# Attention and a channel MLP on one core: v's load, the mixing's staging tiles, V's low part and the pace of weight conversion rearranged

## The chip, the cores and the metric

One core of one Trainium2 chip runs the whole program. The metric is device time in microseconds. Engines: PE is TensorE (PEld its weight loads), DVE VectorE, ACT ScalarE, POOL GpSimd, SP SyncE, which here only issues DMAs. Each engine runs its instructions in program order.

## The reference

Inputs are q, k, v (4 x 8 heads x 576 x 64), a small network w1, b1, w2 for the positional bias, and for the second half U (576 x 32), V (32 x 576), w_ch1 (512 x 2048) and w_ch2 (2048 x 512) in 64-bit floats. All arithmetic is to be good to about float32.

```python
scores = q @ k.T / 8 + bias            # bias[h, i, j] = relu(x[i, j] * w1 + b1) @ w2, the same for every batch
attn = softmax(scores)                 # divided by (sum + 1e-9)
x = (attn @ v) as (4, 576, 512)
h = x.T @ U @ V                        # mixing over the sequence, rank 32
u = x + h.T
out = u + relu(u @ w_ch1) @ w_ch2
```

where x[i, j] = log1p(|i - j|) / log1p(max(i, 1)).

## The kernel before, in words

Products that need float32 precision are made of two parts of 32-bit floats, a rounded high part and the rest, its low part: high*high + high*low + low*high. So every operand is split once, a cast for the high part and a subtraction for the low part.

**Bias stage.** The bias is made first, in 36 steps of 16 rows each (list `order`): `bias_hid` writes four hidden tiles, one on ACT and three on DVE (L312, L314), from a ring of ten slots; `bias_mm` multiplies them on PE; `bias_out` scales the result on ACT into one of eight ring slots (L336) and SP issues two or four DMAs from there to the bias tiles. Four of these eight slots lie in the space of x_sb. Into these steps are set the splits of the first two pairs of heads (`prep_ops(p, True)`: cast on ACT L195, subtraction on DVE L201), the raw loads of pair 1 (`second`), the loads of v, and the first scores, bias adds and exponentials of pair 0 (dictionary `early`). After the steps a memset of 64 rows of x_sb on POOL (L913) waits until the ring's slots in x_sb are read out.

**Attention.** There are 16 pairs of heads, p = 0 to 15, four to a batch. A pair takes one run through the string table SLOTS, nine slots s = 0 to 8 written by hand, in which every name is one step: S scores on PE, T bias add with row minimum on DVE (L385), E exponential on ACT (L403), X and C transposes of P and their copies, I and CI the same for the middle rows, PM `norm_m` (the normalised middle rows, L424 on POOL; for p = 0 on ACT, L422), AV the product with v, A and D assembling x_sb. One prime on a name means the pair before, two the one before that. Q1 to Q4 on POOL split the next pair's q and k (L197, L201); LA and LB issue the raw loads of pair p + 2 on SP. `load_v(p + 1)` is issued at slot 7 of pair p, into one of two v tiles; the tile is free when the step AV1'' of slot 0 has run.

**Conversion.** U, V and the first quarter of the MLP's weights are converted from 64-bit words in 20 jobs, two a pair from pair 2 on (VA, VD, VS, VJ, VP in SLOTS): two ACT steps, three DVE steps (L224, L229, L235), one POOL addition (L240), then a finishing step, which `convert` runs at the next job's VP. For V (three jobs, `fin_v`) this is a cast on ACT (L798) and a DVE instruction (L799) that leaves the high part in some groups of 32 rows and the low part in the others. Converted weights go to DRAM and come back late (`first_weights`, L929, steps listed in FEED).

**Mixing.** When the four pairs of a batch are done, the mixing of that batch runs inside the next pair (p = 5, 9, 13): MT to MX make the rank-32 products, H0 to H4 the five products with V, HD0 to HD4 (`mix_add`, L600) add x_sb into a staging tile y, U0 to U4 (`mix_store`, L604) store it to u_dram. The staging tiles are three, th, tl and y, in turn. The fourth batch's mixing runs in the transition behind the last pair.

**MLP.** u_dram comes back in 18 tiles acc of 128 rows, nine blocks of 256 rows. `make_ut` transposes a block on PE and splits it (ACT L721, DVE L727); `mlp1(n)` makes the hidden layer in four steps and splits it (L763, L764); `mlp2(n)` has two steps, accumulates into acc (L784) and in the last round stores. Weights are handled in four quarters, so there are four rounds of nine blocks (n = 0 to 35). In rounds 1 to 3 the next quarter's weights are converted in `background`: `pipeline` turns 16 jobs into 51 groups of instructions, and after every step of the MLP two groups are issued. All PSUM accumulators come from four tiles of two banks.

The functions of kernel and helpers that the change touches:

Of the kernel before, what the change touches and what calls it, by code (L numbers as in the profile page):

```python
# [20 lines left out]
DM = H * D  # L21
# [25 lines left out]
    "S1 HD3' U3' T1 VA0",  # L47
    "S2 T2 X20' H4' Q1 VP1' Q2 LA C20' HD4' U4'",
    "S3 T3 PM H1' H0' X30' Q3",
# [16 lines left out]
def kernel(  # L66
# [50 lines left out]
    three, mask = consts[:, 2:3].bitcast(I32), consts[:, 3:4].bitcast(I32)  # L117
    low = consts[:, 4:5]
    u_sb = mix.tile([P, 5, RANK], F32, name="u_sb")
# [64 lines left out]
    def prep_ops(p, early=False):  # L184


        hi = qkp.tile([P, 2 * KD * TB], F32R, tag="hi", name="hi")
        lo = qkp.tile([P, QKW], F32R, tag="lo", name="lo")
        qk_ops[p] = (hi, lo)

        parts = [(raws[p, 0], hi[:, 0:QQ], lo[:, 0:QQ]), (raws[p, 1], hi[:, QQ:QKW], lo[:, QQ:QKW])]

        def high(raw, h, l):
            if early:
                nc.scalar.copy(out=h, in_=raw)  # L195
            else:
                nc.gpsimd.tensor_scalar(out=h, in0=raw, scalar1=1.0, scalar2=0.0, op0=ALU.mult, op1=ALU.add)  # L197

        def low(raw, h, l):
            eng = nc.vector if early else nc.gpsimd  # L200
            eng.tensor_tensor(out=l, in0=raw, in1=h.bitcast(F32), op=ALU.subtract)  # L201

        return [lambda o=o, i=i: o(*parts[i]) for i in range(2) for o in (high, low)]
# [49 lines left out]
    small_sb = tabp.tile([P, 33], F32, name="small_sb")  # L253
    extra = tabp.tile([P, S], F32, name="extra")
    psi = tabp.tile([P, S // 32, STEP], F32, name="psi")
# [159 lines left out]
    def norm_m(p):  # L415
# [3 lines left out]
        for o, i, n in ((0, 0, S), (S, S - LEFT, LEFT)):  # L419
            src = d["praw"][:, i : i + n]  # L420
            if p == 0:
                nc.scalar.activation(out=pm[:, o : o + n], in_=src, func=AF.Copy, scale=rec)  # L422
            else:
                nc.gpsimd.tensor_scalar(  # L424
                    out=pm[:, o : o + n], in0=src, scalar1=rec, scalar2=1.0, op0=ALU.mult, op1=ALU.mult
                )

# [119 lines left out]
    mixt = {}  # L547
    stages = cycle(("th", "tl", "y"))

# [47 lines left out]
    def mix_add(c):  # L597
        n = P if c < 4 else LEFT
        y = mixt["y", c] = mix.tile([P, DM], F32, tag=next(stages), name="y")
        nc.vector.tensor_tensor(out=y[0:n], in0=mixt[c][0:n], in1=x_sb[0:n, c, :], op=ALU.add)  # L600
# [6 lines left out]

    conv = {}

    def convert(what, k, p):  # L610
# [12 lines left out]
        elif what == "J":  # L623
            join()
            if j + 3 < len(conv["jobs"]):
                conv["jobs"][j + 3][0]()
        else:
            if j:
                conv["jobs"][j - 1][2]()
            add()  # L630
            if j == len(conv["jobs"]) - 1:
                fin()
# [163 lines left out]
    def fin_v(a, e):  # L796
        def fin(y):
            nc.scalar.copy(out=vq[:, a:e], in_=y)  # L798
            nc.vector.scalar_tensor_tensor(  # L799
                out=vq[:, a:e], in0=vq[:, a:e].bitcast(F32), scalar=low, in1=y, op0=ALU.mult, op1=ALU.add  # L800
            )

# [47 lines left out]
    nc.gpsimd.memset(eps, 1.0e-9)  # L850
    nc.gpsimd.memset(low, 0.0)
    for r in (RANK, 3 * RANK):
        nc.gpsimd.memset(low[r : r + RANK], -1.0)
    load_pair(0)
# [22 lines left out]
    order = [32, 33, 34, 35] + [8 * c + i for c in range(4) for i in (0, 4, 1, 5, 2, 6, 3, 7)]  # L877
    early = {12: 0, 22: 1, 23: 2, 30: 3, 31: 4, 36: 5, 37: 6}
    preps[-1] = prep_ops(0, True)
    second = pair_loads(1)  # L880
    for i in range(len(order) + 3):
# [10 lines left out]
        if 2 <= i < len(order) + 2:  # L892
            bias_out(order[i - 2])
        if i == 25:
            preps[0] = prep_ops(1, True)
        if 5 <= i < 9 or 25 <= i < 29:
            preps[-1 if i < 9 else 0].pop(0)()
        if i in (12, 14, 16, 18, 20, 22):
            second.pop(0)()
        if i == 15:  # L900
            load_v(0)
        if i - 1 in early:
            first(f"E{early[i - 1]}")
        if i - 1 == 12:
            first("N0")
        if i in early:
            first(f"S{early[i]}", f"T{early[i]}")
    load_v(1)
    done.update((f"Q{i}", 0) for i in range(1, 5))
# [28 lines left out]
    for p in range(NP):  # L938
        if p > 0:
            new_pair(p)  # L940
        for s in range(9):
            if s == 7 and 0 < p < NP - 1:
                load_v(p + 1)
            if p == CONV_FROM - 1 and s in (0, 2, 4):
# [29 lines left out]

    period(NP, 0)
    for i in range(6, 9):
# [6 lines left out]
    make_ut(0, 0)  # L983
    period(NP, 1)
    make_ut(0, 1)
    run(m[0][0])
    t = [qkp.tile([P, QKW], F32R, tag="lo", name="ut") for _ in range(2)]
# [28 lines left out]
    for i, c in enumerate((4, 0, 1, 2, 3)):  # L1016
        run((m[2][1:] + y[1])[i])
        last_mix(c)
    p1.close()

# [14 lines left out]
    for n in range(2, NG * NB + 1):  # L1035
# [7 lines left out]
        if g + 1 < NG and (n == 2 or (j == 0 and g > 0)):  # L1043
            queue += pipeline(weight_jobs(g + 1, split))
            queue[1:1] = [[]] * 8
        steps = []
        if n + 1 < NB:
            steps += [lambda i=i: make_ut(n + 1, i) for i in range(TT)]
        if 2 < n < NG * NB:
            steps += mlp1(n)  # L1050
        if n > 2:
            steps += mlp2(n - 1)
        for o in steps:
            o()
            background(2)

# [69 lines left out]
```

## Time and profile before

| | |
|---|---|
| median of 3 runs | 745.96 us (742.02 to 750.25) |
| the profiled execution | 745.49 us, span 743.5 us |
| PE busy, share of the span | 696.8 us, 94% |
| DVE, ACT, POOL busy | 60%, 48%, 28% |
| mean granted TensorE clock | 0.982 |
| bias stage, with pair 0's first scores | 5.3 to about 76 us |
| attention, pairs 1 to 15 | to about 309 us |
| transition to the MLP | to about 355 us |
| MLP, conversion of the second quarter beside it | 354.9 to 434.4 us |
| MLP, the three rounds left | to 743.5 us |

The span is from the first to the last instruction. PE's busy time has the overlap of its pipelined matmuls modelled, so a stage at 100% is a stage in which PE never waits, at whatever clock.

### The profile page before, as it was taken

Reading aid. Unit: us, or ns where it says so; the run is one execution under the profiler, and the core shown is the slowest. Engines: PE = TensorE matmul, PEld = TensorE weight load, DVE = VectorE, ACT = ScalarE, POOL = GpSimd, SP = SyncE. Lnnn points to the kernel's source line nnn. Section 1 sums busy time; section 2 is a strip of 40 time slices with the busy share of each in tenths; the row PEclk is TensorE's granted clock in tenths of the full one; section 3 lists DMA queues with packets and bytes.
Section 4 is the critical chain, followed back from the end, with each engine's and each line's share of the span. In section 5 each row is a group of like instructions: output and inputs, shape, how many; then the busy total and the mean of one; then the engine's idle time right before and its main releaser. Section 6 shows DMA issues by size and latency. Waiting matters only on the chain.

```text
span 743.5 us, 16699 instructions
## 1 busy us (share of the span) xinstructions
PE 696.8 (94%) x6708; PEld 573.4 (77%) x6708; DVE 447.4 (60%) x932; ACT 358.7 (48%) x769; POOL 207.8 (28%) x225
## 2 busy tenths in 40 slices
PE   6978898889999998899899999999999999999998
PEld 4434676657766776687787989989989989989986
DVE  7977698879988877334598328842268622222222
ACT  7978798769987987631355114421044211011010
POOL 0000565445664645200166005520036400000000
PEclk9999999999999999999999999999999999999999
DMA  5687645454554454301533002310013000011111
GB/s 131 190 209 205 155 120 141 112 155 127 162 163 124 124 140 153 118 2 50 202 100 106 6 1 88 91 50 1 1 55 102 30 1 1 1 42 43 57 44 71
DMA packets 39885, 68.25 MB, mean 92 GB/s; under 512 B 5888, under 2 KB 12544, under 8 KB 39808
## 3 DMA queue, kind: packets, MB, share of 16 engines
q1 hardware_dynamic: 39424, 67.01, 31.0%
q8 instruction: 53, 0.87, 0.5%
q14 instruction: 24, 0.20, 0.1%
q10 hardware_dynamic: 384, 0.18, 0.1%
HBM read 45.02 MB, written 11.53 MB: 76 GB/s over the span
## 4 chain that ended last, share of the span: by engine, by line
PE 76%; DMA 6%; DVE 6%; ACT 4%; issue 3%; SPq 2%; POOL 2%; DVEq 0%; POOLq 0%; ACTq 0%
PE ph L758 25%; PE po L781 25%; PE o L505 10%; PE sc L370 7%; PE tb L447 3%; DMA bias<-ring 2%; DMA u_dram<-y 2%; PE bs L321 2%; PE tx L447 1%; DVE ring L314 1%; DMA raw<-in_qk_dram 1%; PE ti L447 1%; ACT ring L312 1%; DVE wt L235 1%; DVE wt L229 1%
## 5 line engine op out<-in xcount | busy, mean ns | idle before, releaser
L763 ACT ACTIVATE hh<-ph 128x1024 fp32r<-128x1024 f32 x36 | 36.9, 1025 | 203.3 <-PE ph L758 203.3
L764 DVE SCALAR_TENSOR_TENSOR hh<-ph,hh 128x1024 fp32r<-128x1024 f32 x36 | 44.1, 1225 | 139.1 <-ACT hh L763 139.1
L240 POOL TENSOR_TENSOR wy<-wt,wy 128x256 int32<-128x256 int32 (+1 forms) x68 | 52.5, 772 | 234.8 <-DVE wt L235 197.0
L781 PE MATMUL po<-bias,hh 128*128 128x512 f32 x432 | 102.1, 391 | 0.0
L403 ACT ACTIVATE p<-p,st 128x576 f32<-128x576 f32 x128 | 98.3, 771 | 2.9 <-DVE st L385 2.9
L781 PE MATMUL po<-wq,hh 128*128 128x512 f32 x360 | 98.1, 394 | 0.0
L385 DVE CUSTOM_DVE_ANT_0 p<-sc,bias 128x576 f32<-128x576 f32 x128 | 92.6, 750 | 8.4 <-PE sc L370 4.7
L505 PE MATMUL o<-pt,v 128*64 128x320 f32 (+1 forms) x640 | 87.8, 422 | 5.1 <-DVE y L600 5.1
L781 PEld LDWEIGHTS po<-bias,hh 128*128 128x128 f32 x432 | 79.8, 188 | 16.2
L781 PEld LDWEIGHTS po<-wq,hh 128*128 128x128 f32 x360 | 66.6, 188 | 14.3
L505 PEld LDWEIGHTS o<-pt,v 128*64 128x64 f32 x640 | 44.3, 141 | 36.1 <-DVE y L600 5.5
L758 PE MATMUL ph<-ut,bias 128*128 128x256 f32 x512 | 67.5, 280 | 2.7 <-DVE bias L784 2.7
L758 PEld LDWEIGHTS ph<-ut,bias 128*128 128x128 f32 x512 | 63.8, 189 | 3.6 <-issue 3.1
L758 PE MATMUL ph<-ut,wq 128*128 128x256 f32 x512 | 65.0, 276 | 0.0
L758 PEld LDWEIGHTS ph<-ut,wq 128*128 128x128 f32 x512 | 62.0, 188 | 1.0
L201 POOL TENSOR_TENSOR lo<-raw,hi 128x1152 fp32r<-128x1152 f32 (+1 forms) x28 | 59.3, 2117 | 1.5
L370 PE MATMUL sc<-hi 64*128 64x288 f32 (+1 forms) x320 | 57.1, 349 | 2.7 <-DVE y L600 1.9
L321 PE MATMUL bs<-ring,small_sb 128*32 128x256 f32 (+2 forms) x780 | 50.6, 367 | 8.4 <-ACT ring L312 7.3
L430 ACT COPY pt<-tb 128x1024 f32<-128x1024 f32 x48 | 47.9, 1012 | 16.1 <-PE tb L447 16.1
L784 DVE TENSOR_TENSOR acc<-po,acc 128x512 f32<-128x512 f32 x36 | 24.9, 691 | 46.4 <-PE po L781 46.4
L758 PE MATMUL ph<-bias 128*128 128x256 f32 x352 | 51.1, 290 | 1.2 <-ACT bias L721 0.7
L370 PE MATMUL sc<-lo,hi 64*128 64x288 f32 (+1 forms) x320 | 49.2, 299 | 0.6 <-POOL lo L201 0.6
(110 smaller groups left out, 1217.2 us busy)
## 6 DMA issues: line engine op xcount, KB each, us to landing
wraw<-in_w_ch_dram SPq DMA_DIRECT2D x64, 256.0 KB
raw<-in_qk_dram SPq DMA_DIRECT2D x32, 288.0 KB
bias<-ring SPq DMA_DIRECT2D x64, 144.0 KB
v<-in_vp_dram SPq DMA_DIRECT2D x16, 320.0 KB
u_dram<-y SPq DMA_DIRECT2D x16, 256.0 KB
raw<-in_qk_dram SPq DMA_DIRECT2D x32, 88.0 KB
raw<-in_qk_dram SPq DMA_DIRECT2D x32, 72.0 KB
bias<-u_dram SPq DMA_DIRECT2D x9, 256.0 KB
```

The lines of the kernel that those rows point to most:

```text
L201: eng.tensor_tensor(out=l, in0=raw, in1=h.bitcast(F32), op=ALU.subtract)
L240: nc.gpsimd.tensor_tensor(out=st["y"], in0=st["t"], in1=st["y"], op=ALU.add)
L321: mm(bs[T][32 * cg : 32 * cg + 32, a, o : o + n], lhsT=w2_sb, rhs=hids[T][cg][:, i : i + n], start=True, stop=True, tile_position=(0, 32 * ...
L370: mm(ps[0:n, a, 0:HALF], lhsT=q[r, q0 : q0 + n], rhs=k[r, k0 : k0 + HALF], start=(i == 0), stop=(i == len(terms) - 1),)
L385: nc.vector.tensor_tensor_reduce(out=halves(dst), in0=d.pop(("ps", s))[:, :, 0:HALF], in1=halves(bias_at(p % HP, s)), scale=-0.125, scalar ...
L403: nc.scalar.activation(out=dst, in_=dst, func=AF.Exp, bias=st[:, s : s + 1], scale=-1.0, accum_out=st[:, 10 + s : 11 + s])
L430: nc.scalar.copy(out=out, in_=in_)
L447: nc.tensor.transpose(bank[:, h, i * D : (i + 1) * D], src[r, a : a + P], ident[r, r])
L505: mm(o[hd * D : (hd + 1) * D, 0:n], lhsT=v[:, vb * D : (vb + 1) * D], rhs=pt[:, pb, :], start=(j == 0), stop=(j == 4),)
L758: mm(d, lhsT=w, rhs=u, start=(i == 0), stop=(i == 3 * KD - 1))
L764: nc.vector.scalar_tensor_tensor(out=hl[n], in0=st["ps"], scalar=0.0, in1=hh[n].bitcast(F32), op0=ALU.max, op1=ALU.subtract)
L781: mm(ps, lhsT=h, rhs=w, start=(m == 0), stop=(m == 3 * FG - 1))
```

## The change

- **SLOTS:** LA (two raw loads of pair p + 2 on SP) moves behind C20' HD4' U4' in slot 2.
- **Early splits:** the casts of the first two pairs go from ACT to POOL; the subtractions stay on DVE.
- **norm_m(0)** goes from ACT to POOL, as for the other pairs.
- **Bias steps:** pair 1's raw loads are issued in steps 9 to 14 (before: 12, 14, ... 22), its split runs in steps 22, 23, 25, 26 (before: 25 to 28), and the first scores come one to three steps earlier.
- **v:** `load_v(p)` is issued at slot 3 of its own pair. Before, v of pairs 0 and 1 were loaded in the bias stage and the others one pair earlier.
- **Mixing:** y takes five tiles in turn: the space of table, that of extra, y, th, tl.
- **V's low part:** two POOL subtractions of 32 rows each per job in place of DVE's instruction, issued behind the next job's addition (list `late`). The constant `low` and its three memsets go.
- **Transition:** `period(16, 0)` moves behind `make_ut(0, 0)` and `make_ut(0, 1)`; `period(16, 1)`, in which no step is due, goes. `make_ut(3, ...)` moves into the last mixing's steps.
- **First round:** for n = 3 the transposes of block 4 come behind `mlp1(3)`; the queue of conversion starts without eight empty groups; one group is issued after a step (two after the first of each n). Later rounds keep two.

```diff
@@ SLOTS
-    "S2 T2 X20' H4' Q1 VP1' Q2 LA C20' HD4' U4'",
+    "S2 T2 X20' H4' Q1 VP1' Q2 C20' HD4' U4' LA",
@@ prep_ops
         def high(raw, h, l):
-            if early:
-                nc.scalar.copy(out=h, in_=raw)
-            else:
-                nc.gpsimd.tensor_scalar(out=h, in0=raw, scalar1=1.0, scalar2=0.0, op0=ALU.mult, op1=ALU.add)
+            nc.gpsimd.tensor_scalar(out=h, in0=raw, scalar1=1.0, scalar2=0.0, op0=ALU.mult, op1=ALU.add)
@@ norm_m
-            if p == 0:
-                nc.scalar.activation(out=pm[:, o : o + n], in_=src, func=AF.Copy, scale=rec)
-            else:
-                nc.gpsimd.tensor_scalar(
-                    out=pm[:, o : o + n], in0=src, scalar1=rec, scalar2=1.0, op0=ALU.mult, op1=ALU.mult
-                )
+            nc.gpsimd.tensor_scalar(
+                out=pm[:, o : o + n], in0=src, scalar1=rec, scalar2=1.0, op0=ALU.mult, op1=ALU.mult
+            )
@@ mixing
-    stages = cycle(("th", "tl", "y"))
+    stages = cycle([(tabp, "tab"), (tabp, "extra"), (mix, "y"), (mix, "th"), (mix, "tl")])
...
-        y = mixt["y", c] = mix.tile([P, DM], F32, tag=next(stages), name="y")
+        pool, tag = next(stages)
+        y = mixt["y", c] = pool.tile([P, DM], F32, tag=tag, name="y")
@@ convert, the VP step
         else:
+            lows = late[:]
+            del late[:]
             if j:
                 conv["jobs"][j - 1][2]()
             add()
+            for o in lows:
+                o()
@@ fin_v
             nc.scalar.copy(out=vq[:, a:e], in_=y)
-            nc.vector.scalar_tensor_tensor(
-                out=vq[:, a:e], in0=vq[:, a:e].bitcast(F32), scalar=low, in1=y, op0=ALU.mult, op1=ALU.add
-            )
+            for r in (RANK, 3 * RANK):
+                o = vq[r : r + RANK, a:e]
+                late.append(
+                    lambda o=o, y=y[r : r + RANK]: nc.gpsimd.tensor_tensor(
+                        out=o, in0=y, in1=o.bitcast(F32), op=ALU.subtract
+                    )
+                )
@@ bias steps
-    early = {12: 0, 22: 1, 23: 2, 30: 3, 31: 4, 36: 5, 37: 6}
+    early = {11: 0, 19: 1, 21: 2, 28: 3, 30: 4, 36: 5, 37: 6}
...
-        if i == 25:
+        if i == 22:
             preps[0] = prep_ops(1, True)
-        if 5 <= i < 9 or 25 <= i < 29:
+        if 5 <= i < 9 or i in (22, 23, 25, 26):
             preps[-1 if i < 9 else 0].pop(0)()
-        if i in (12, 14, 16, 18, 20, 22):
+        if 9 <= i < 15:
             second.pop(0)()
-        if i == 15:
-            load_v(0)
...
-    load_v(1)
@@ pairs
-            if s == 7 and 0 < p < NP - 1:
-                load_v(p + 1)
+            if s == 3:
+                load_v(p)
@@ transition
-    period(NP, 0)
...
     make_ut(0, 0)
-    period(NP, 1)
     make_ut(0, 1)
+    period(NP, 0)
     run(m[0][0])
...
         last_mix(c)
+        if i > 2:
+            make_ut(3, i - 3)
@@ MLP
-            queue[1:1] = [[]] * 8
-        steps = []
-        if n + 1 < NB:
-            steps += [lambda i=i: make_ut(n + 1, i) for i in range(TT)]
-        if 2 < n < NG * NB:
-            steps += mlp1(n)
+            queue[1:1] = [[]] * (8 if n > 2 else 0)
+        steps = mlp1(n) if 2 < n < NG * NB else []
+        if 2 < n < NB - 1:
+            feed = [lambda i=i: make_ut(n + 1, i) for i in range(TT)]
+            steps = steps + feed if n == 3 else feed + steps
         if n > 2:
             steps += mlp2(n - 1)
-        for o in steps:
+        for i, o in enumerate(steps):
             o()
-            background(2)
+            background(2 if n >= NB or i == 0 else 1)
```

## Rows read from the trace of the kernel before

**Rows 1.** Windows by stage: length; busy PE, PEld, DVE, ACT, POOL; PEclk; DMA share; GB/s

```profile
96.00:109.20 13.20, 13.01 (x194) 10.11 (x195) 12.88 (x35) 12.89 (x32) 6.80 (x7) 1.00 0.42 119
109.20:142.90 33.70, 28.83 (x388) 22.73 (x388) 30.55 (x73) 27.30 (x70) 20.26 (x20) 0.90 0.48 129
142.90:177.90 35.00, 31.53 (x411) 22.20 (x411) 27.83 (x75) 25.81 (x61) 14.07 (x13) 0.95 0.45 135
204.20:239.10 34.90, 31.64 (x409) 22.24 (x409) 29.25 (x76) 26.62 (x65) 17.47 (x17) 0.95 0.50 144
264.90:282.40 17.50, 17.20 (x215) 11.68 (x215) 13.93 (x36) 14.53 (x34) 6.65 (x6) 1.00 0.56 164
282.40:298.70 16.30, 13.12 (x194) 10.06 (x194) 11.13 (x33) 12.65 (x30) 7.52 (x8) 1.00 0.40 137
354.90:434.40 79.50, 72.93 (x470) 66.06 (x471) 48.39 (x77) 28.29 (x65) 26.07 (x32) 0.98 0.30 97
434.40:501.10 66.70, 66.70 (x434) 60.42 (x434) 43.40 (x66) 22.91 (x54) 26.51 (x32) 1.00 0.21 64
```

**Rows 2.** Timeline of DVE, 40 to 76 us: start, us, instruction, [idle before <-releaser]

```profile
45.94 0.95 DVE L314 TENSOR_SCALAR ring<-tab,psi_b 128x576 f32<-128x576 f32 x2 [0.97 <-PE bs L321]
49.07 1.36 DVE L201 TENSOR_TENSOR lo<-raw,hi 128x1152 fp32r<-128x1152 f32 x1 [2.18 <-ACT hi L195]
54.81 0.82 DVE L201 TENSOR_TENSOR lo<-raw,hi 128x640 fp32r<-128x640 f32 x1 [1.80 <-ACT hi L195]
75.12 0.76 DVE L385 CUSTOM_DVE_ANT_0 p<-sc,bias 128x576 f32<-128x576 f32 x1 [2.27 <-DMA bias<-ring]
```

**Rows 3.** Groups by line and shape: busy us, mean ns of one, idle before

```profile
L197 POOL TENSOR_SCALAR hi<-raw 128x1152 fp32r<-128x1152 f32 x14 | 16.2, 1160 | 23.0 <-PE sc L370 7.0 <-DMA raw<-in_qk_dram 6.7 <-DVE wt L224 5.0
L197 POOL TENSOR_SCALAR hi<-raw 128x640 fp32r<-128x640 f32 x14 | 11.1, 790 | 0.0
```

**Rows 4.** Timeline of POOL, 72 to 86 us

```profile
75.80 0.53 POOL L913 MEMSET x_sb<- 64x512 f32 x1 [70.88 <-DMA bias<-ring]
84.51 1.06 POOL L424 TENSOR_SCALAR pm<-praw,st 128x576 f32<-128x576 f32 x2
```

**Rows 5.** Timeline of PE, 71 to 76 us

```profile
71.60 0.37 PE L447 MATMUL ti<-ident,pm 64*128 64x64 f32 x2 [2.67 <-ACT pm L422]
75.03 0.29 PE L370 MATMUL sc<-hi,lo 64*64 64x288 f32 x2
```

**Rows 6.** Timeline of DVE, 112 to 140 us

```profile
119.59 2.08 DVE L799 SCALAR_TENSOR_TENSOR vq<-vq,eps,wy 128x256 fp32r<-128x256 f32 x1 [0.81 <-ACT vq L798]
135.79 2.71 DVE L799 SCALAR_TENSOR_TENSOR vq<-vq,eps,wy 128x128 fp32r<-128x128 f32 x1 [0.58 <-ACT vq L798]
```

**Rows 7.** Timeline of POOL, 135 to 139 us

```profile
135.73 2.63 POOL L201 TENSOR_TENSOR lo<-raw,hi 128x1152 fp32r<-128x1152 f32 x1
```

**Rows 8.** Waits over the span: us in total, times, longest us

```profile
DVE y L600 <- DMA u_dram<-y: 6.9, 5, 3.0
```

**Rows 9.** Timeline of SP's DMA queue, 290 to 292 us

```profile
290.81 0.33 SPq L182 DMA_DIRECT2D v<-in_vp_dram  x1
291.23 0.86 SPq L929 DMA_DIRECT2D y<-wq_dram  x2
```

**Rows 10.** Timeline of PE, 298 to 359 us

```profile
298.33 0.40 PE L447 MATMUL tx<-ident,ot 64*128 64x64 f32 x6 [2.93 <-ACT pt L430]
309.37 0.39 PE L758 MATMUL ph<-bias 128*128 128x256 f32 x1 [0.73 <-ACT bias L721]
358.04 1.09 PE L719 MATMUL tu<-ident,acc 128*128 128x128 f32 x4 [3.15 <-DMA acc<-u_dram]
```

**Rows 11.** Timeline of ACT, 364 us

```profile
364.51 0.44 ACT L217 ACTIVATE wt<-wraw 128x256 f32<-128x256 f32 x1 [4.77 <-DMA wraw<-in_w_ch_dram]
```

**Rows 12.** Groups by line and shape, the MLP's hidden layer

```profile
L763 ACT ACTIVATE hh<-ph 128x1024 fp32r<-128x1024 f32 x36 | 36.9, 1025 | 203.3 <-PE ph L758 203.3
L764 DVE SCALAR_TENSOR_TENSOR hh<-ph,hh 128x1024 fp32r<-128x1024 f32 x36 | 44.1, 1225 | 139.1 <-ACT hh L763 139.1
```

More of the change, by code (lines that the diff above doesn't have):

```diff
@@ L117 @@
     three, mask = consts[:, 2:3].bitcast(I32), consts[:, 3:4].bitcast(I32)
-    low = consts[:, 4:5]
     u_sb = mix.tile([P, 5, RANK], F32, name="u_sb")
@@ L253 @@
     small_sb = tabp.tile([P, 33], F32, name="small_sb")
-    extra = tabp.tile([P, S], F32, name="extra")
+    extra = tabp.tile([P, S], F32, tag="extra", name="extra")
     psi = tabp.tile([P, S // 32, STEP], F32, name="psi")
@@ L606 @@
     NP = B * HP
-    conv = {}
+    conv, late = {}, []
     def convert(what, k, p):
@@ L850 @@
     nc.gpsimd.memset(eps, 1.0e-9)
-    nc.gpsimd.memset(low, 0.0)
-    for r in (RANK, 3 * RANK):
-        nc.gpsimd.memset(low[r : r + RANK], -1.0)
     load_pair(0)
@@ L893 @@
             bias_out(order[i - 2])
-        if i == 25:
+        if i == 22:
             preps[0] = prep_ops(1, True)
-        if 5 <= i < 9 or 25 <= i < 29:
+        if 5 <= i < 9 or i in (22, 23, 25, 26):
             preps[-1 if i < 9 else 0].pop(0)()
-        if i in (12, 14, 16, 18, 20, 22):
+        if 9 <= i < 15:
             second.pop(0)()
-        if i == 15:
-            load_v(0)
         if i - 1 in early:
             first(f"E{early[i - 1]}")
-        if i - 1 == 12:
+        if i - 1 == 11:
             first("N0")
```

## The prediction

> **What bounds the kernel now.** I read the windows by stage first, because the shares of the whole page mix four stages. In a pair of heads that only converts weights beside its attention (96.0 to 109.2 us), TensorE is busy 13.01 of 13.20 us, VectorE 12.88 and ScalarE 12.89 [rows 1]: three engines end together, and nothing is to be had there. The stages that stand out against 13.2 a pair are the two pairs that convert V (33.70 for two), the two pairs at each of the first two mixings (35.00 and 34.90 for two), the pair before the last (16.30) and the MLP's first round: 79.50 us with TensorE busy 72.93, where the next round takes 66.70 and is busy throughout [rows 1]. The third mixing, by contrast, has TensorE busy 17.20 of 17.50 [rows 1]; it can give nothing. Ahead of them lies the bias stage, whose end is a transfer. I then asked for the timelines around these places, to see which wait comes last in each. The reader is to see that nearly every place is an in-order queue standing behind one late thing.
>
> **Bias stage and first pair.** The change takes four casts and the two products of norm_m(0) from ScalarE, spreads the first scores two or three steps earlier, and issues pair 1's raw loads in six steps running, without v between them. What VectorE loses there is three waits, 0.97 + 2.18 + 1.80 = 4.95 us, two of them for ScalarE's cast of a raw tile that came late [rows 2]. With the raws ordered ten steps earlier I count these as gone. The casts are now GpSimd's, 1.16 and 0.79 us for each of two pairs, 3.9 in all [rows 3]. GpSimd was idle, so they cost nothing by themselves, but VectorE's rows beside them may be held: none at all, or all 3.9. No row shows a one-input VectorE instruction against GpSimd, so I take half, 1.95. The last ring transfer, E, landed at about 75.80 before; it comes 4.95 - 1.95 = 3.0 earlier (bounds 1.05 and 4.95).
>
> Against this stands what is queued behind norm_m(0) on its new engine, or rather ahead of it. GpSimd's memset of x_sb waits for E: it started at 75.80, after 70.88 us of waiting [rows 4]. norm_m(0) comes after it in GpSimd's program. Its pair took 1.06 for another p [rows 4], so the pm tile is complete at E + 0.53 + 1.06 = E + 1.6. TensorE already waited 2.67 us for pm until 71.60, and is in order: from there to the last scores of the pair it took until 75.03 + 0.29 = 75.32, 3.7 us, with S7 and S8 among it [rows 5]. Now that chain ends at E + 5.3, where before VectorE could add the last bias at about E (it was already past its 2.27 us wait for a ring transfer at 75.12 [rows 2]). So the first pair ends up to 5.3 later against E; if TensorE does its part at full clock, some 3.8. I take 4.8. The stage nets 3.0 - 4.8 = **-1.8**, between -4.2 and +1.1.
>
> **V's low part.** Its three VectorE instructions lasted 2.08 and 2.71 us in the two rows shown, after 0.81 and 0.58 of waiting for ScalarE's cast [rows 6]. Of them the wider one is the shorter: the row of 2.71 runs beside a GpSimd subtraction of 2.63 that began 0.06 earlier [rows 7] and ends with it. Taking these out, VectorE's 30.55 falls to under 26 of 33.70, and ScalarE's 27.30 becomes the bound [rows 1]. With its usual gaps of 0.3 a pair that makes 27.9, or 5.8 saved. On GpSimd six subtractions, at most 256 wide, join 20.26 us of work [rows 1]; by the 1152-wide one of 2.63 they take some 0.6 to 0.7 each, 4 together, which fits, and one conversion later the cast is mostly done. Two of them stand ahead of the next pair's lo in GpSimd's queue and make it at most 1.4 late, about the room that the pair's end has. I take **+5.5** (bounds 3.7 and 7.3, the last if both pairs return to 13.2).
>
> The Trainium skill bears on this ("SBUF — State Buffer", section "Who interferes with whom"): a VectorE instruction with two SBUF inputs, or in a two-port mode, and a GpSimd instruction that reads SBUF exclude each other for the whole instruction. The rows of 2.71 and 2.63 agree. By the same rule the casts of the bias stage would hold VectorE for their full length; the rival below has what that makes.
>
> **Mixing.** y now cycles through five tiles, one for each store of a mixing, and LA no longer stands ahead of U4's store on SP. VectorE's waits for u_dram stores come to 6.9 us in five times over the span [rows 8], nearly all in the first two mixings. A floor for two pairs is 26.4 plus the mixing's own TensorE time, 17.20 - 13.12 = 4.1 (the windows of the third mixing and of the pair behind it): 30.5 against 35.00 and 34.90, so 8.9 in all; the granted clock of 0.95 there, below the 1.00 of the plain pair [rows 1], is a part of it that goes with the waits. The waits alone give 6.6. VectorE has 27.83 and 29.25 of work in these windows, close to the floor, so I take **+7.6**. What is late next is TensorE itself. The tiles called tab and extra are idle by then; if they weren't, the first stores would wait as the third did.
>
> **v in its own pair.** In steady pairs SP merely waits at another place: nothing is gained, and LA, whose raws were never last in a plain pair, hides its shift. Before the last pair it matters: the v load stood on SP until 290.81, and two loads of converted weights only went out at 291.23 [rows 9]; ScalarE waited for them with a copy of pt behind, and TensorE 2.93 us at 298.33 for that [rows 10]. Now the first can go early, the second when its buffer is free, which no row here dates: 1.0 to 2.9, and I take **+2.2**. v for the last use comes many steps ahead of AV and costs nothing; if it were late, AV would wait for about one landing.
>
> **Into the MLP.** Having period(16, 0) behind both transposes covers a wait of 0.73 us [rows 10] with attention work: **+0.7** (bounds 0 and 0.7). The removed period(16, 1) issues nothing.
>
> **First round.** TensorE lost 79.50 - 72.93 = 6.6 us, plus the granted clock's 2% [rows 1], 1.6, together 8.2. Of this 3.15 was one wait for acc [rows 10], with mlp1(3) behind it; now mlp1(3) runs first and covers it. The others belong to conversion groups queued on VectorE ahead of the hidden layer, at two a step; one a step should leave few. But with no empty groups ahead, the first raw load is issued and awaited in the same step, and ScalarE stood for it until 364.51 [rows 11]. The load goes out behind nine acc loads as before, so it lands no earlier. Behind it on ScalarE stands the activation of mlp1(3), for which VectorE and then PSUM wait: of four PSUM buffers ph, two tu and one po are taken, so the second po of mlp2(2) needs ph's. Two conversion steps of 0.44, the activation of 1.03 and VectorE's part of 1.23 [rows 12] make ph free some 3.1 us after 364.51, at 367.6. TensorE starts at 354.9 + 0.7, needs 5.6 for mlp1 (a twelfth of 66.70), 0.9 for the transposes and 2.8 for the first po, and is there at 364.9: a wait of 2.7, with perhaps 1.6 of lower clock behind it. New losses 0.7 + 2.7 + 1.6 = 5.0, and 8.2 - 5.0 = 3.2; I take **+3.0** (bounds 0 and 7.5). The queue empties in time: 51 groups against 52 places to the end of the round.
>
> **Sum.** -1.8 + 5.5 + 7.6 + 2.2 + 0.7 + 3.0 = 17.2; the span goes from 743.5 to 726.3. The profiled run took 745.49, 2.0 outside the span, and lies 0.5 under the median of 745.96, so I forecast **728 us**.
>
> **Rivals.**
> 1. The start gains: E moves the full 4.95, and ScalarE, freed of casts, absorbs all but 2 of norm_m's delay; and the first round finds its PSUM buffer in time (+6.5). That is 3.0 + 5.5 + 7.6 + 2.2 + 0.7 + 6.5 = 25.5, **720 us**. For it speaks that these two are my only costs; against it that both come from program order.
> 2. GpSimd holds VectorE for all of the four casts: E moves 1.05 only, and the time is **730 us**. For it the two instructions of [rows 6, 7]; against it that VectorE's instruction there reads two SBUF tensors and L314 reads one. The page named above gives this result if L314 counts as a two-port instruction.
> 3. The removed waits are replaced: ScalarE or VectorE, at 12.9 of 13.2, can't take up more, and V's and the mixings' pairs return 2.5 and 3.3. The sum is 9.9, **736 us**. Against it that the third mixing ran at 17.50 with the same mixing work, though without conversions.
> 4. The change doesn't do what it says: a staging tile still waits for a store or for an old reader, and the mixings give nothing: 9.6, **736 us**.
> 5. Slower: in the first round each popped group holds TensorE a little, and there are now 51 steps with a group where there were about 30. At 0.5 us a group this costs 25.5 against 14.2 gained elsewhere, **757 us**; it makes the kernel slower from about 0.28 us a group. Against it: the second round converts two groups a step with TensorE idle for nothing [rows 1].
>
> **How the numbers follow.** Chances: forecast 0.45, rival 1 0.17, rival 2 0.18, rival 3 0.12, rival 4 0.05, rival 5 0.03. My bounds all at their worst give 738, all at their best 717; the range of 718 to 737 leaves out only the extreme ends and rival 5. A difference under 1%, 7.5 us, can hardly be told from none in this kernel; so faster needs 738.5 or less, which all but rival 5 and the far ends of 3 and 4 give: 0.93 faster, 0.05 same, 0.02 slower.
>
> **What would show it.** The V pairs at about 14 us each and no VectorE row of V's; the mixing windows at 31 and no wait of y for u_dram; weights for the last pair issued before 290 relative to it; TensorE's wait for pm longer than before and released by GpSimd after the memset; a wait of TensorE in the first po pair after mlp1(3). The prediction fails if the bias stage ends much earlier or later than E - 3, or if the pairs move to ScalarE's bound elsewhere.

## The result, and the profile after

The changed kernel takes **726.21 us** (median of 4 runs, 724.9 to 726.99) against 746.86 for the kernel before on the same chip: ratio 0.9726, 95% interval 0.9669 to 0.9784. Forecast were 728 in a range of 718 to 737. The profiled execution took 726.99 with a span of 725.1, 18.4 less than before's 743.5, where the terms had added up to 17.2.

The sum can be right with wrong terms, so the stages come first. A good mark of a pair is the start of its first AV product on TensorE (o<-pt,v, 128x320). The table takes it from the timelines of both kernels; "n=9" is the first product of the MLP's second round. It lists the time between marks.

| stretch | before | after | gain | forecast |
|---|---|---|---|---|
| start to second AV0 | 95.93 | 98.48 | -2.55 | -1.8 |
| the two pairs of V | 33.70 | 28.56 | +5.14 | +5.5 |
| first and second mixing, two pairs each | 34.97, 34.95 | 31.47, 30.30 | +8.15 | +7.6 |
| pair before the last | 16.24 | 14.19 | +2.05 | +2.2 |
| from there to the last AV0 | 28.17 | 25.08 | +3.09 | +0.7 |
| last AV0 to n=9 | 107.39 | 106.03 | +1.36 | +3.0 |
| all other pairs | | | +1.17 | 0 |

Windows by stage of the changed kernel: start:end, length, then busy time of TensorE, its weight loads, VectorE, ScalarE and GpSimd, the granted clock, DMA share and GB/s. They answer to [rows 1]: a plain pair, V, the two mixings, the third mixing, the pair before the last, the blocks n = 3 to 8 of the first round, and the next six blocks, n = 9 to 14. (The prediction calls the last of these stretches "the next round"; a round has nine blocks.)

```profile
98.50:111.10 12.60, 12.60 (x196) 9.83 (x194) 11.84 (x35) 12.60 (x32) 5.70 (x7) 1.00 0.33 90
111.10:139.60 28.50, 27.00 (x386) 20.22 (x384) 27.63 (x69) 25.94 (x66) 20.31 (x22) 1.00 0.51 131
139.60:171.10 31.50, 30.70 (x411) 22.04 (x407) 30.92 (x76) 27.04 (x65) 18.84 (x18) 1.00 0.59 169
197.20:227.50 30.30, 30.30 (x411) 21.91 (x407) 29.38 (x76) 26.90 (x65) 17.31 (x17) 1.00 0.59 166
253.30:270.50 17.20, 17.20 (x217) 11.76 (x215) 13.92 (x36) 14.23 (x34) 6.93 (x5) 1.00 0.57 158
270.50:284.80 14.30, 13.20 (x197) 10.14 (x196) 11.01 (x32) 12.89 (x30) 7.83 (x9) 1.00 0.59 210
338.10:416.00 77.90, 73.79 (x474) 66.56 (x475) 45.88 (x77) 27.95 (x64) 24.90 (x32) 0.96 0.31 99
416.00:482.00 66.00, 66.00 (x430) 59.86 (x430) 43.44 (x66) 22.89 (x54) 26.51 (x32) 1.00 0.21 65
```

The reader is to see two things. The granted clock, 0.90 to 0.95 in the V and mixing windows of before, is 1.00 in all of them now, and TensorE's idle time there, 4.9, 3.5 and 3.3 us before, is 1.5, 0.8 and none. So the second mixing has TensorE busy for the whole 30.30, and it has reached the floor of 30.5 that the prediction named. The first round is the exception: shorter by little, with a lower clock than before. VectorE's waits for stores to u_dram [rows 8] are gone; of the waits of y this one is left (us in total, times, longest):

```profile
DVE y L594 <- PE mh L588: 1.6, 2, 1.0
```

Bias stage. These rows of the changed kernel's timelines (start, us, instruction, idle before and its releaser) answer to [rows 2, 4, 5].

```profile
35.63 1.44 POOL L193 TENSOR_SCALAR hi<-raw 128x1152 fp32r<-128x1152 f32 x1 [23.27 <-DMA raw<-in_qk_dram]
74.48 0.52 POOL L909 MEMSET x_sb<- 64x512 f32 x1 [32.23 <-DMA bias<-ring]
75.10 1.05 POOL L417 TENSOR_SCALAR pm<-praw,st 128x576 f32<-128x576 f32 x2
```

```profile
76.20 0.37 PE L440 MATMUL ti<-ident,pm 64*128 64x64 f32 x2 [8.58 <-POOL pm L417]
```

```profile
35.96 1.42 DVE L310 TENSOR_SCALAR extra<-tab,psi_b 128x576 f32<-128x576 f32 x1
39.17 0.76 DVE L381 CUSTOM_DVE_ANT_0 p<-sc,bias 128x576 f32<-128x576 f32 x1 [1.79 <-DMA raw<-in_qk_dram]
46.16 1.35 DVE L197 TENSOR_TENSOR lo<-raw,hi 128x1152 fp32r<-128x1152 f32 x1
78.30 0.76 DVE L381 CUSTOM_DVE_ANT_0 p<-sc,bias 128x576 f32<-128x576 f32 x1 [0.84 <-PE sc L366]
```

norm_m(0) stands behind the memset and TensorE waits 8.58 us for it, as forecast. VectorE's waits for hi are gone (46.16 has no idle), but two others have come: a hidden-layer instruction at 35.96, beside GpSimd's cast of 35.63, lasts 1.42 where its like lasts 0.51, and one of the first scores waits 1.79 at 39.17. The trace names a raw load as its releaser; the instruction reads scores and bias and no raw tile, so I take it that it waits for its bias rows, which come over the same queue. In runs 1 and 2 below the trace names a raw load in the same way. VectorE's last hidden layer ends at 65.06 here and at 66.10 before, 1.0 earlier, and the memset starts 1.32 earlier.

First round, answering to [rows 10, 11]: the same kind of rows for SP's queue, ScalarE, VectorE and TensorE.

```profile
338.63 4.35 SPq L712 DMA_DIRECT2D acc<-u_dram  x9
343.08 2.17 SPq L206 DMA_DIRECT2D wraw<-in_w_ch_dram  x3
```

```profile
348.94 0.43 ACT L213 ACTIVATE wt<-wraw 128x256 f32<-128x256 f32 x1 [10.86 <-DMA wraw<-in_w_ch_dram]
349.59 1.01 ACT L761 ACTIVATE hh<-ph 128x1024 fp32r<-128x1024 f32 x1
```

```profile
350.78 1.22 DVE L762 SCALAR_TENSOR_TENSOR hh<-ph,hh 128x1024 fp32r<-128x1024 f32 x1
```

```profile
345.29 3.03 PE L779 MATMUL po<-bias,hh 128*128 128x512 f32 x12
352.05 5.42 PE L779 MATMUL po<-bias,hh 128*128 128x512 f32 x12 [3.73 <-DVE hh L762]
```

This is the chain that the prediction wrote down, row by row: SP issues the raws behind nine acc loads, ScalarE stands for the first raw with the activation behind it, VectorE's half of the hidden layer follows, and the second output tile waits 3.73. Then the same twelve products take 5.42 instead of 3.03, at a granted clock of 0.51 (the lower of the two levels, 1.2 GHz), as the window over them shows:

```profile
352.00:357.40 5.40, 5.35 (x13) 4.16 (x14) 3.35 (x6) 1.72 (x5) 2.21 (x3) 0.51 0.32 95
```

### The profile page after: what moved, and what is told of

It reads as the page before. It is cut to its first block, busy times and chain, and to the rows that moved or that the text cites. A ratio compares the mean times of both kernels' runs of the same rounds, so it can differ in the third digit from the quotient of the medians.

```text
span 725.1 us, 16712 instructions
## 1 busy us (share of the span) xinstructions
PE 692.3 (95%) x6708; PEld 575.9 (79%) x6708; DVE 446.5 (62%) x929; ACT 354.6 (49%) x763; POOL 216.8 (30%) x234
## 4 chain that ended last, share of the span: by engine, by line
PE 85%; DVE 5%; ACT 3%; DMA 3%; issue 2%; SPq 1%; POOL 0%; DVEq 0%; ACTq 0%; POOLq 0%
PE po L779 28%; PE ph L756 27%; PE o L498 10%; PE sc L366 9%; PE tb L440 4%; PE bs L317 2%; DVE ring L310 2%; DMA bias<-ring 1%; PE mh L588 1%; ACT p L399 1%; PE tx L440 1%; PE ti L440 1%; DMA wraw<-in_w_ch_dram 1%; PE tu L717 1%; DVE wt L220 1%
## 5 line engine op out<-in xcount | busy, mean ns | idle before, releaser
L779 PE MATMUL po<-bias,hh 128*128 128x512 f32 x432 | 105.0, 398 | 3.7 <-DVE hh L762 3.7
L779 PEld LDWEIGHTS po<-bias,hh 128*128 128x128 f32 x432 | 81.3, 192 | 20.7 <-DVE hh L762 4.2
L498 PE MATMUL o<-pt,v 128*64 128x320 f32 (+1 forms) x640 | 84.7, 411 | 0.1
L317 PE MATMUL bs<-ring,small_sb 128*32 128x64 f32 (+2 forms) x780 | 51.1, 355 | 5.3 <-DVE ring L310 2.4
L756 PE MATMUL ph<-bias 128*128 128x256 f32 x352 | 48.5, 282 | 0.7 <-ACT bias L719 0.7
```

Of the source, the lines that this page charges most:

```text
L317: mm(bs[T][32 * cg : 32 * cg + 32, a, o : o + n], lhsT=w2_sb, rhs=hids[T][cg][:, i : i + n], start=True, stop=True, tile_position=(0, 32 * ...
L498: mm(o[hd * D : (hd + 1) * D, 0:n], lhsT=v[:, vb * D : (vb + 1) * D], rhs=pt[:, pb, :], start=(j == 0), stop=(j == 4),)
L756: mm(d, lhsT=w, rhs=u, start=(i == 0), stop=(i == 3 * KD - 1))
L779: mm(ps, lhsT=h, rhs=w, start=(m == 0), stop=(m == 3 * FG - 1))
```

## The experiments

Each is one edit on the changed kernel, or several where the heading says so. The executions of one kernel differ by 0.9 us (runs 2 and 9) to 8.5 (run 6), so small effects are read from the marks of the profiled execution, one for each kernel, and the medians stand beside them. Two comparisons set the scale. First, seven kernels here have the same bias stage as the change (it itself and the runs on the raw loads, the values' old instruction, three tiles, LA, the two parts undone and the late subtractions). Their memset, which starts when the last ring transfer has landed, starts at 74.48, 74.81, 75.64, 74.54, 73.55, 74.21 and 75.12. A shift of under 2 us there shows nothing. Second, nine kernels have the same first round (the change and runs 1 to 4 and 6 to 9). From the last AV0 to n=9 they take 106.03, 106.26, 102.67, 104.80, 104.85, 105.58, 105.80, 104.06 and 105.43, on average 105.05: the wait before the second output tile is 2.83 to 4.15 us in them, and the tile behind it takes 3.02 to 5.49. The change's own execution, to which the runs below are compared, is near the slow end.

**1. The memset behind norm_m(0).**

```
-    nc.gpsimd.memset(x_sb[D:P, 4, :], 0.0)      # ahead of all pairs
+            if (p, s) == (0, 3):                # after period(p, s)
+                nc.gpsimd.memset(x_sb[D:P, 4, :], 0.0)
```

> Edit: the memset of x_sb stands behind norm_m(0) in GpSimd's program instead of ahead of it. Theory (norm_m(0) is late only because the memset ahead of it waits for the last ring transfer): pm is complete at about 70 us instead of 76.15, TensorE goes on to S7 and S8 without the 8.6 us wait, VectorE adds the bias of T7 at about 74.5, when the last ring transfer has landed, instead of 78.30, and the second AV0 moves from 98.48 to about 94.7: 3.8 us, about 722.5. Rival: the first pair ends by ScalarE, busy 12.27 of 12.50 us in the stretch behind, and the gain is under 1 us.

Measured: 723.33 us, ratio 0.9708 (0.9658 to 0.9758); second AV0 at 94.32 instead of 98.48. Rows of this run:

```profile
68.97 1.05 POOL L417 TENSOR_SCALAR pm<-praw,st 128x576 f32<-128x576 f32 x2 [26.88 <-DVE st L409]
74.53 0.52 POOL L943 MEMSET x_sb<- 64x512 f32 x1 [4.51 <-DMA raw<-in_qk_dram]
```

```profile
73.84 0.76 DVE L381 CUSTOM_DVE_ANT_0 p<-sc,bias 128x576 f32<-128x576 f32 x1 [2.52 <-DMA bias<-ring]
```

VectorE's T7 again waits for the bias and for nothing else, as before the change [rows 2]. The mark moves 4.16, of which up to 0.6 is the earlier landing: the order on GpSimd costs 3.5 to 4.2, and nothing behind absorbs it. By the medians it is 2.9, within the uncertainty of either.

**2. The casts on ScalarE again**, and **3. the first scores at their old steps**, and **4. both.**

```
         def high(raw, h, l):
+            if early: nc.scalar.copy(out=h, in_=raw)      # runs 2 and 4
...
-    early = {11: 0, 19: 1, 21: 2, 28: 3, 30: 4, 36: 5, 37: 6}
+    early = {12: 0, 22: 1, 23: 2, 30: 3, 31: 4, 36: 5, 37: 6}   # runs 3 and 4
...
-        if i - 1 == 11:
+        if i - 1 == 12:                                          # runs 3 and 4
             first("N0")
```

> Edit: the four casts of the bias stage are ScalarE's again, all else as changed. Theory (GpSimd's casts hold VectorE's one-input instructions: by the trace of the changed kernel 1.3 us at 10 to 12.4, 0.9 at 36 and 0.46 at 41.5, 2.7 in all): VectorE's rows beside them are 0.51 and 0.95 again and the memset that waits for the last ring transfer starts about 2.7 us earlier than 74.48, at 71.8; the time falls by 2 to 2.7, to 723.5 to 724.5. Rival 1: ScalarE comes late with the casts, VectorE waits for hi by about what the hold was, and the memset starts within 0.5 of 74.48. Rival 2: the wait of 1.79 for bias rows at 37 us sets the stage, and only the part behind it (0.5 us) is gained.

> Edit: the first scores stand at their old steps of the bias stage again (12, 22, 23, 30, 31); casts stay on GpSimd, the raw loads at their new places. Theory (VectorE's wait for the bias rows at 37 us, 1.79 with GpSimd's casts and 3.80 without, sets the stage): the wait goes and the memset that waits for the last ring transfer starts 1.5 to 1.8 earlier than 74.48, at about 72.8. Rival (the stage ends by SP, which issues 86 transfers at 0.6 us each and lies some 4 us behind ScalarE at its end): the memset starts within 0.5 of 74.48, and the time stays at 726.

> Edit: the casts of the bias stage on ScalarE and the first scores at their old steps, so that of this part of the change only the earlier raw loads and norm_m(0) are left. Theory (the wait for bias rows and GpSimd's hold of VectorE together set the stage): the memset starts 3.8 to 4.4 earlier than 74.48, at 70.1 to 70.7; against the kernel with old steps and GpSimd's casts the difference is the hold, 2.7. Rival (SP's issues set it): within 0.7 of 74.48, as both others.

Measured: 723.5 us (0.9717, 0.9673 to 0.976), 723.63 (0.9705, 0.9665 to 0.9745) and 725.53 (0.9725, 0.9691 to 0.976). Memset at 74.45, 73.63 and 74.28. One row of VectorE from the timeline of run 2, and the last group of hidden-layer instructions in those of the change, of run 3 and of run 4:

```profile
39.94 0.76 DVE L384 CUSTOM_DVE_ANT_0 p<-sc,bias 128x576 f32<-128x576 f32 x1 [3.80 <-DMA raw<-in_qk_dram]
```

```profile
63.68 1.38 DVE L310 TENSOR_SCALAR ring<-tab,psi_b 128x576 f32<-128x576 f32 x3
```

```profile
61.34 1.38 DVE L310 TENSOR_SCALAR ring<-tab,psi_b 128x576 f32<-128x576 f32 x3
```

```profile
61.51 1.56 DVE L313 TENSOR_SCALAR ring<-tab,psi_b 128x576 f32<-128x576 f32 x3
```

With the casts away VectorE is not held (rows of 0.51 and 0.52 throughout), but its wait for the bias rows grows from 1.79 to 3.80 and takes the gain. With the scores moved back the wait is gone and VectorE is done with the hidden layers 2.0 to 2.3 us earlier (by the ends of these groups). The last transfer lands when it did. The theories of all three runs fall, and what holds is the rivals' common part, that the memset stays; run 3's 0.85 is inside the spread. Run 2's time of 723.5 is what its theory forecast, but not by its reason: its second AV0 is at 98.38, and 3.4 of the 3.5 us by which its span is the shorter lie in the first round (102.67 against 106.03), where the second output tile took 3.02 behind a wait of 2.99, at full clock. **VectorE does not set the end of the bias stage** in the changed kernel: 8.7 to 11.2 us lie between its last hidden layer and the landing in these kernels. In the kernel before this gap is 9.7; no run tests it there. Nor does ScalarE seem to: with the casts back on it, in runs 2 and 4, the landing stays, and in run 3 its last copy into the ring ends 2.3 us earlier (65.49 against 67.82).

**5. The first raws ahead of the acc loads.**

```
+    queue += pipeline(weight_jobs(1, split))
+    background(1)                  # the three raw loads
+    queue.insert(0, [])            # later groups keep their steps
     for i in range(9, NT // P):    # acc loads
```

> Edit: the first three raw loads of the first round's conversion are issued ahead of its nine acc loads; the conversion's steps stay where they are. Theory (ScalarE's wait of 10.9 us for the first raw delays the hidden layer's activation, and so TensorE's second output tile by 3.73 us, with lower clock behind it): the raw lands before mlp1(3) is done at 344.8, the hidden layer is complete at about 347.0, TensorE doesn't wait at 348.3, and the output tile takes about 2.9 instead of 5.42: 6.2 us less, about 720. Rival 1: the wait goes and the clock falls elsewhere: 3.7 less, 722.5. Rival 2: the acc loads now land 1 to 2 us later and TensorE waits for them at the transposes of 344.9 instead: 2 to 3 less, about 724.

Measured: **720.18 us**, ratio 0.9674 (0.9628 to 0.972). Last AV0 to n=9 takes 99.36 instead of 106.03: 6.67 less, or 5.7 less than the average of the nine kernels above. Runs 11 and 12, which have the same edit, take 99.31 and 99.42. A row of TensorE's timeline in this run, and its window over the same products:

```profile
345.39 5.73 PE L779 MATMUL po<-bias,hh 128*128 128x512 f32 x24
```

```profile
345.40:351.00 5.60, 5.60 (x28) 4.57 (x26) 4.57 (x7) 3.28 (x9) 1.48 (x2) 1.00 0.86 321
```

Both output tiles run without a break, at full clock. The wait and the clock behind it go together, and the acc loads, issued 1.5 us later (340.11), hold nobody.

**6. The values' low part on VectorE again.** The edit is the reverse of the change in fin_v.

> Edit: the low part of the values is VectorE's single instruction over all partitions again, in its old place; all else as changed. Theory (that instruction and its waits cost the two pairs of V what the marks say): the two pairs from the fourth to the sixth AV0 go from 28.5 to about 33.7 us, and the time is 5.2 higher, about 731.5. Rival: part of the 33.7 came from other things that the change took away from these pairs (LA's place, v's load), and only 2 to 3 us come back, 728 to 729.

Measured: 730.72 us (726.42 to 734.92), ratio 0.9792 (0.9733 to 0.9852); the two pairs took 35.93 in the profiled execution, the slowest of the four. Three rows of VectorE's timeline in this run:

```profile
122.49 2.06 DVE L798 SCALAR_TENSOR_TENSOR vq<-vq,eps,wy 128x256 fp32r<-128x256 f32 x1 [0.81 <-ACT vq L797]
125.89 0.94 DVE L798 SCALAR_TENSOR_TENSOR vq<-vq,eps,wy 128x256 fp32r<-128x256 f32 x1
141.05 2.70 DVE L798 SCALAR_TENSOR_TENSOR vq<-vq,eps,wy 128x128 fp32r<-128x128 f32 x1 [0.59 <-ACT vq L797]
```

The rows of [rows 6] are back to 0.02 us. By the medians the part is worth 4.5, by the marks of the slowest execution 7.4; the theory's 5.2 lies between. The rival's 2 to 3 is under both, but the four executions spread over 8.5 us and don't exclude it.

**7. The subtractions behind the next low part.**

```
-            for o in lows:
-                o()
+            ready.extend(lows)      # run behind Q2, the query's long low part
```

> Edit: the values' subtractions on GpSimd stand behind the next low part of the key instead of ahead of it. Theory (in the two pairs of V they push GpSimd's long subtraction, 2.67 us, onto VectorE's conversion instructions, which take 1.5 to 2.1 instead of 0.5 there): these instructions are short again and the two pairs take about 26.5 to 27 instead of 28.5: 724 to 724.5. Rival: the two engines exclude each other as long as GpSimd subtracts, at whatever place, and the two pairs take 28.5 plus or minus 0.5.

(Q2 makes the low part of q, 1152 wide; the expectation calls it the key's.) Measured: 729.65 us, ratio 0.9778 (0.9732 to 0.9824): worse. The pairs took 13.58 and 17.87 instead of 13.61 and 14.95. In the first of them VectorE's conversion instructions are short again, 0.37 and 0.74 where the change has these:

```profile
124.09 2.12 DVE L220 SCALAR_TENSOR_TENSOR wt<-wt,eps 128x256 f32<-128x256 f32 x1
128.42 1.58 DVE L231 SCALAR_TENSOR_TENSOR wt<-wraw,sgn,wt 128x256 int32<-128x256 int32 x1
```

and yet what came out is no shorter. In the second, this run's list of waits (engine and tile, releaser, us in total, times, longest) has

```profile
ACT wy L216 <- POOL vq L803: 4.3, 1, 4.3
PE sc L366 <- ACT pt L423: 4.2, 2, 4.0
```

The delayed subtraction holds its source tile, ScalarE wants that buffer for the next conversion, and TensorE waits for ScalarE's copy. Neither theory had that. The edit shows that the subtractions can't be put off freely; what bounds the V pairs at 28.5 instead of 26.4 stays open.

**8. Three staging tiles, LA moved**, and **9. five tiles, LA in its old place.**

```
-    stages = cycle([(tabp, "tab"), (tabp, "extra"), (mix, "y"), (mix, "th"), (mix, "tl")])
+    stages = cycle([(mix, "th"), (mix, "tl"), (mix, "y")])             # run 8
-    "S2 T2 X20' H4' Q1 VP1' Q2 C20' HD4' U4' LA",
+    "S2 T2 X20' H4' Q1 VP1' Q2 LA C20' HD4' U4'",                      # run 9
```

> Edit: the mixing's y cycles through three tiles again; LA keeps its new place behind U4's store. Theory (a staging tile that waits for a store of the same mixing cost VectorE 6.6 us): waits of y for u_dram come back, the first two mixing stages (marks of AV0 after 139.65 and 197.24) take about 34.5 and 34 instead of 31.5 and 30.3, and the time is 6 to 7 higher, 733. Rival: LA's place on SP's queue made the stores late before, and with LA moved three tiles are nearly enough: 2 us or less, 727 to 728.

> Edit: LA stands ahead of U4's store again; five staging tiles stay. With three tiles and LA behind, one wait of 1.41 us came back and the first mixing took 2.7 longer, so LA's move gave the larger part or each of the two edits covers the other. Theory (each covers the other: with a tile for each store no store can hold VectorE, wherever it is issued): the mixing stages take 31.5 and 30.3 as with the whole change, no wait of y for u_dram, 726. Rival (SP's place of LA by itself costs the mixings): they take 33 and 32 or more, 729 to 731.

Measured: run 8 728.01 us, ratio 0.9758 (0.9722 to 0.9795), the mixings 34.13 and 30.17; run 9 725.84 us, 0.9727 (0.9688 to 0.9767), 31.46 and 30.18. The one wait that is left in run 8, from VectorE's timeline:

```profile
157.63 0.69 DVE L594 TENSOR_TENSOR y<-mh,x_sb 128x512 f32<-128x512 f32 x1 [1.41 <-DMA u_dram<-y]
```

With five tiles LA's place makes no difference. With three tiles and LA moved 2.66 of the 8.15 is missing; whether LA's move gives the other 5.5 is not shown, since no run undoes both. So neither edit can be called the cause of the 8.15 by itself; the prediction named both and priced the tiles. Run 8's theory fell, and run 9's held.

**10. Two parts undone that lie in different stages**: the first round as before, and v one pair ahead.

> Edit: two parts undone that lie in different stages: the MLP's first round is the old one (eight empty groups, two groups a step, transposes ahead), and v is loaded one pair ahead at step 7 again. Theory from the marks: the pair before the last takes 16.2 instead of 14.2 with TensorE's wait of 2.9 for pt back (+2.0), the mixings stay (five tiles cover them), and the stretch from the last AV0 to n=9 gets 1.5 longer: 729.5 to 730. Rival on the round: the new order is worth the 3.0 that I took, and part of it went to the wait for the hidden layer; then 731. Rival on v: no effect at the pair before the last, since converted weights wait for their buffer anyway.

Measured: 731.1 us, ratio 0.9798 (0.9758 to 0.9838). The pair before the last takes 16.02, the stretch to the last AV0 26.35, from there to n=9 108.12. Windows of the first two, and the wait between them:

```profile
270.14:286.16 16.02, 13.26 (x196) 10.14 (x193) 11.12 (x33) 13.17 (x30) 8.41 (x11) 0.97 0.46 150
286.16:312.51 26.35, 25.89 (x267) 21.34 (x265) 10.16 (x22) 15.31 (x34) 3.62 (x3) 0.95 0.21 67
```

```profile
285.64 0.58 PE L440 MATMUL tx<-ident,ot 64*128 64x64 f32 x6 [2.52 <-ACT pt L423]
```

v's place is worth 1.83 in its pair and 1.27 behind it, where the clock is 0.95 after the wait and was 1.00 without it. The round's new order is worth 2.1 against the change's execution, and 3.1, as the rival had it, against the average of the nine. With the 2.1 the parts make 5.2 together, against 4.9 by the medians. The mixings stay at 31.46 and 30.19, so v's place isn't needed for them.

**11. Three edits together** (those of runs 1, 3 and 5), and **12. pair 1's raws on GpSimd's queue as well.**

```
-    second = pair_loads(1)
+    second = pair_loads(1, nc.gpsimd)          # run 12
```

> Edit: the memset behind norm_m(0), the first raw loads of the first round ahead of the acc loads, and the first scores at their old steps, all on the changed kernel. By the marks of the single runs 4.16 (98.48 to 94.32), 6.2 and 0.85: 715. Rival: with TensorE busier its clock falls and 2 to 3 us come back, 717 to 718.

> Edit: as the kernel with three edits, and pair 1's six raw loads of the bias stage are issued by GpSimd instead of SP. Theory (the end of the bias stage is set by SP, which issues 86 transfers one after the other at about 0.6 us): the last ring transfer lands 3 to 3.7 us earlier, T7 starts near 70.5, and the time is 3 to 3.7 under that of the kernel with three edits. Rival (DMA engines, at 0.71 of their time, or VectorE's 60 of 69 us set it): T7 moves by less than 1 us.

Measured: run 11 **718.01 us** (716.85 to 719.13), ratio 0.9625 (0.9593 to 0.9658); run 12 **715.14** (714.59 to 718.9), 0.9589 (0.9553 to 0.9625). Both lie below the change's interval. Run 11's median is 8.2 under the change's, its profiled execution 10.1 (716.85 against 726.99), where the marks had promised 11.2. One part of that is plain: its second AV0 is at 94.88, not at 94.32 less 0.85, so run 3's 0.85 was spread and no gain. The rival's time came out, but not by its reason: TensorE's clock is 1.00 from 334.5 to 405.4 in this run.

Run 12's profiled execution is the slowest of its six and shows no gain: T7 at 75.74. SP has 64 transfers in a row there, without the six raws:

```profile
21.26 50.75 SPq L338 DMA_DIRECT2D bias<-ring  x64
```

That is 0.79 us each, where the change issues 46 in 32.52, 0.71 each, and two of them in 1.18 where they don't queue, 0.59 each. So SP stands in these 50.75 us too, the issues aren't its bound in that execution, and the theory falls there. The median is 2.9 lower than run 11's all the same, though the intervals overlap, and no profile of these faster runs exists; the four fastest have a mean granted clock of 0.996 to 0.997, where run 11's six have 0.989 to 0.995. What ends the bias stage stays open. Left are the transfers themselves, which no run tests: between 40 and 72 us the kernels move 200 to 208 GB/s, in before 206, in the change 208, in runs 11 and 12 206 and 200.

## Why the prediction was right, point by point

**Start, -1.8 (measured -2.55).** Half right, and nearer in sum than in its halves: E gave 1.7 less than forecast and norm_m(0) cost less too. norm_m(0) behind the memset was named with its queue and priced at 4.8; run 1 gives 3.5 to 4.2. The other half, "The last ring transfer, E, landed at about 75.80 before; it comes 4.95 - 1.95 = 3.0 earlier", is the step that failed: E came 1.32 earlier, less than the spread of 2.1. The hold by GpSimd's casts was there, 2.7 by the rows (1.3 at 10 us, 0.9, 0.46) against 1.95, and the earlier first score brought a wait of 1.79 that I had not counted. But runs 2 to 4 show that even without either E doesn't move: VectorE's waits aren't on the path to it. A wait that was read as a loss had room behind it. What does end the stage stays open. On the hold, the Trainium skill ("SBUF — State Buffer", section "Who interferes with whom") says that tensor_scalar, where its operands allow it, can enter a two-port mode and then shuts out GpSimd, or is shut out, for the whole instruction; the row of 1.42 against 0.51 agrees.

**V, +5.5 (5.14; 4.5 by run 6).** Right in size, not in the path. The working said that VectorE falls under 26 and ScalarE becomes the bound; VectorE has 27.63 and ScalarE 25.94 of 28.5, so VectorE is still the busier. VectorE's conversion instructions run into GpSimd's delayed subtraction, and run 7 shows that taking this away does not shorten the first of the two pairs.

**Mixing, +7.6 (8.15).** Right, by the mechanism given: no store holds VectorE, and the second mixing is at TensorE's floor. That without the added tiles, but with LA moved, only 2.66 would be missing was not seen.

**v load, +2.2, and entry, +0.7 (2.05 and 3.09).** The wait is as read; the term was too small by the clock behind it. Before, TensorE ran at 0.94 from 298.7 to 326.8, and run 10 at 0.95 after its wait of 2.52: v is worth 3.1. The remaining 2.0 of the two stretches is the entry's wait and its part of the same clock, which no run separates.

**First round, +3.0 (1.36; 2.3 by the average of the nine kernels; 2.1 to 3.1 by run 10).** The mechanism was right and the wait was mis-sized. The raw came 10.8 us after the round began, where I had 9.6, which made a wait of 3.73 of my 2.7 (3.4 on average in the nine). The clock behind it cost 2.4 here (5.42 against 3.03) where I had put 1.6; in the nine it cost from nothing to 2.5, on average 1.7, so that size was right and this execution a bad one. The new losses in it are 0.68 + 0.34 + 3.73 + 2.4 = 7.1, not 5.0. Run 5 takes back 6.0 to 6.7 of them with a load issued 4.4 us earlier.

**What made up for it.** The terms fell short by 0.75 and 1.64 at the start and in the round and by 0.36 and 0.15 at V and v, and were exceeded by 0.55 and 2.39 in the mixings and at the entry. The other pairs gave 1.17 that had no term. So the sum is within 1.2 us because shortfalls of 2.9 and excesses of 2.9 cancelled, and that is luck. The mixings, v's load and the first round are right by their mechanism, V in size only, and the start by half; at the entry no run separates the parts. The range held because it was wider than the errors.

**The rivals.** Rival 1's first round exists (run 5 takes 99.36 where the kernel before took 107.39, 8.0 less against its 6.5), but it takes another order of loads. Rival 2's hold exists, and E doesn't depend on it. Rivals 3 and 4 are out by the windows: the mixings came down to TensorE's floor. Rival 5 is out: with a group a step TensorE is busy for all of the 57.80 us from 358.0 to 415.8.

## What to carry to other kernels

A wait on an engine is worth something only if that engine ends the stage: ask, before adding up its waits, how long after its last instruction the stage ends (here 9 to 11 us, and no cure of VectorE moved it). When a wait of TensorE is priced, give the clock behind it a range: here it cost 1.27 behind a wait of 2.52, 2.4 behind one of 3.73, and nothing behind one of 2.99 in run 2. And one profiled execution is not the kernel: before a stretch of two kernels is compared, see how far it differs between kernels that share it (here 3.6 us in the first round). And when work moves to an idle engine, look at what already stands at the head of that engine's queue; here an unrelated memset cost some 4 us, and moving it one place back was free.

## What the runs showed of the hardware

- A one-input VectorE instruction beside a GpSimd cast of a single tile lasted 1.42 us instead of 0.51; with the casts on ScalarE all were 0.51 or 0.52.
- After a wait of 3.73 us TensorE's granted clock was 0.51 for the 5.4 us that followed, and 1.00 again behind that; without the wait (run 5) it stayed at 1.00. The fall does not always follow: in run 2 the clock stayed at 1.00 behind a wait of 2.99, in run 8 it was 0.66 for 4.3 us behind one of 2.83.
- The landing of the last ring transfer varies by 2.1 us (73.55 to 75.64) between kernels with the same bias stage, and so does, in part, the whole time.
